# The first two query tiles of q and k by the hardware queues as token pairs, with a new load list and TensorE order

## The chip, the cores and the metric

The kernel runs on one core of one Trainium2 chip. The metric is the device time of one execution in microseconds, as the median of several runs. The profile shown is one execution on that core.

## The reference

Attention with a local window, a few global keys and a linear distance bias, for 4 batches, 8 heads, 768 tokens and a head size of 64, then a feed-forward layer with squared ReLU over 3072 tokens (512 to 2048 to 512). n_global is 8, n_local is 96.

```python
scores = scale * np.matmul(q, k.transpose(0, 1, 3, 2))
is_global = pos[None, :] < int(n_global)
is_local = (rel >= 0) & (rel < int(n_local))
keep = is_global | is_local
dist = np.where(is_global & ~is_local, float(n_local), np.abs(rel).astype(np.float32))
scores = scores - slopes[:, None, None] * dist[None, :, :]
scores = np.where(keep, scores, -1000000000.0)
a = np.exp(scores - np.max(scores, axis=-1, keepdims=True))
a = a / (np.sum(a, axis=-1, keepdims=True) + 1e-09)
attn_out = np.matmul(a, v).astype(np.float32)
x = attn_out.transpose(0, 2, 1, 3).reshape(B * S, H * D)
h = np.maximum(x @ w_in, 0.0)
out = h * h @ w_out
```

## The kernel before

A batch has six query tiles of 128 tokens. Because the window is 96 tokens long and the global keys are the first 8, a query tile needs only two key tiles: its own ("o") and the one before it ("b"), in which the first 32 rows are replaced by those of tile 0 (`kb` for keys, `vb` for values; tile 1 uses tile 0 itself). Three query tiles make a "half"; there are eight halves. The feed-forward layers of one half run on TensorE between the attention steps of the next. Only the first batch is done tile by tile, in an opening of about 25 us; it is what the change touches.

Everything is recorded as operations of a planner, `Plan`. TensorE's operations and the loads of GpSimd keep the order in which they are listed. For the first batch these orders are written by hand in two strings, OPENING and LOADING. The operations of the other engines are put into an order, and given to ScalarE (ACT) or VectorE (DVE), by the planner's costs and due times; on the chip every engine then works through its own fixed order. Where the planner expects TensorE to wait in the opening, `warm` fills the time with matmuls on a zero tile (L217 and L220).

The names in OPENING, for query tile r and half i of the four head pairs:

- `Tr`: `turn_tile`, transposes of a tile of q and k by TensorE into PSUM (L663), eight 128x128; two copies `qk<-trp` bring them to SBUF, and two more (`kb`) build the key tile with the global rows.
- `Sro`, `Srb`: `score_tile`, eight score matmuls of 64 rows (L696). For the tiles 0 to 2 eight more matmuls put the distance bias in (L689), and ACT's exp gives the weights at once; for tiles 3 to 5 VectorE multiplies by a mask after the exp (L717).
- `Ari`: `attend_tile` (L735), and on VectorE the reciprocal of the row sum and the scaling (L745 and L747, "norm" below).
- `Xri`: `tile_to_x`, two transposes (L762), copied into `xt`.
- `Vr`: `fix_v`, two VectorE copies for `vb` (L206). It is no TensorE operation; VectorE does it when its turn comes and waits there for the load.
- `Fc`, `Gci`, `Dc`, `Eci`: pieces of the first layer (L557) for the first tile, the second and third tiles, and the tiles of the second half; `c` is the chunk of w_in that they need.

PSUM is taken from two rings: six large buffers (`big`, for T, S, F, G) and two small ones (`att`, for A and X).

The names in LOADING are tiles of 128 tokens of q, k and v, and the chunks c0 to c3 of w_in. They are cast to float16 by the transfer (L316, L364), whose contiguous piece is one head of one token, 256 bytes. Tile 0 of q and k alone comes by the hardware queues of SP and ACT in float32, in one transfer each (L354), and is cast by VectorE (`sq<-rsq`, `sk<-rsk`). The loads of w_out follow (L371), then those of the next batch.

```python
OPENING = """T0 V2 S0o T1 A00 A01 S1b T2 S1o S2b S2o X00 A11 A10 X11 T3 X10 T4 V1 X01 A20 S3o S3b A21 F0
X20 S4o X21 S4b T5 A30 A31 V3 G01 S5b G00 F1 X30 G11 A41 A40 S5o V4 G10 G20 G21 X41 X31 F2
G31 X40 F3 A50 A51 E10 E01 G30 X50 X51 E11 E00 D0 D1"""
LOADING = """v1 k1 v0 q1 k2 q2 k3 v2 k4 q3 q4 c0 k5 q5 v3 c1 v4 c2 c3 v5"""
```

Of the kernel before, what the change touches and what calls it, by code (L numbers as in the profile page):

```python
# [8 lines left out]
FP32 = mybir.dt.float32  # L9
FP16 = mybir.dt.float16  # L10
# [3 lines left out]
P = 128  # L14
# [2 lines left out]

OPENING = """T0 V2 S0o T1 A00 A01 S1b T2 S1o S2b S2o X00 A11 A10 X11 T3 X10 T4 V1 X01 A20 S3o S3b A21 F0  # L20
X20 S4o X21 S4b T5 A30 A31 V3 G01 S5b G00 F1 X30 G11 A41 A40 S5o V4 G10 G20 G21 X41 X31 F2
G31 X40 F3 A50 A51 E10 E01 G30 X50 X51 E11 E00 D0 D1"""

LOADING = """v1 k1 v0 q1 k2 q2 k3 v2 k4 q3 q4 c0 k5 q5 v3 c1 v4 c2 c3 v5"""

# [29 lines left out]
class Plan:  # L59
# [10 lines left out]
    def __init__(self, warm_from, warm_until):  # L70
        self.warm_from, self.warm_until = warm_from, warm_until
        self.queues = {"PE": [], "LOAD": []}
        self.rest = []
        self.free = {e: 0.75 for e in ("ACT", "DVE", "POOL", "SP")}
        self.landed = 3.4
        self.rank = 0

    def pe(self, cost, emit, needs=(), takes=(), lag=0.24):
# [76 lines left out]
def kernel(  # L155
# [11 lines left out]
    nc = tc.nc  # L167

    B, H, S, D = q.shape
    NG, NL = int(n_global), int(n_local)  # L170
    d_model, d_ff = moe_w_in.shape
    NT = S // P
    NPAIR = H // 2
# [5 lines left out]
    GR = 32  # L179
# [7 lines left out]
    stage_p = ctx.enter_context(tc.tile_pool(name="stage", bufs=2))  # L187
# [4 lines left out]
    y_p = ctx.enter_context(tc.tile_pool(name="yp", bufs=6))  # L192
    ps_big = ctx.enter_context(tc.tile_pool(name="ps_big", bufs=6, space=bass.MemoryType.PSUM))
    ps_att = ctx.enter_context(tc.tile_pool(name="ps_att", bufs=2, space=bass.MemoryType.PSUM))

    plan = Plan(1.0, 24.0)
    big, att = Ring(6), Ring(2)

    def eng(e):
        return {"ACT": nc.scalar, "DVE": nc.vector, "POOL": nc.gpsimd}[e]  # L200

    def copy(e, out, in_):
        if e == "ACT":
            nc.scalar.copy(out=out, in_=in_)  # L204
        else:
            eng(e).tensor_copy(out=out, in_=in_)  # L206
# [5 lines left out]
    def warm(ps):  # L212
        fp32 = ps.dtype == FP32
        n = min(512, ps.shape[-1]) if fp32 else P
        for _ in range(int(plan.spare / (n / 2400 + 0.003))):
            if fp32:
                nc.tensor.matmul(ps[:, 0:n], lhsT=zero[:, 0:P], rhs=zero[:, 0:n], start=True,  # L217
                                 stop=True)
            else:
                nc.tensor.transpose(out=ps[:, 0:n], in_=zero[:, 0:P], identity=ident)  # L220
# [3 lines left out]
    ident = const.tile([P, P], FP16, name="ident")  # L224
# [72 lines left out]
    def behind(dma, first):  # L297
        tc.add_manual_dep(dma.ins, first.ins.name, mybir.DependencyInfo(
            mybir.DependencyClass.Sync, mybir.DependencyReason.DATA), reason="in turn")

    def staged(x, name):
        if getattr(x, name, None) is None:
            setattr(x, name, stage_p.tile([P, HT, H, D], FP16, name=name, tag=name))
        return getattr(x, name)

    def list_loads(x):
        r0 = x.half * HALF
        prev = halves[x.hb - 2] if x.hb >= 2 else None
        before = (prev.turned if prev else []) + ([*halves[x.hb - 1].turned, prev.x_ops[NPAIR - 1]] if x.hb > 3 else [])
        vbefore = [halves[x.hb - x.half - 3].attended[-1]] if x.hb >= 4 else []  # L310

        def rows(src, name, t, rank=None):
            def emit(e):
                dst = (x.bt.v[:, x.half * HT + t, :, 0:D] if name == "v"
                       else staged(x, name)[:, t, :, :])
                dma = nc.gpsimd.dma_start(out=dst, in_=src[x.b, :, r0 + t * P:r0 + (t + 1) * P, :]  # L316
                                          .rearrange("h p d -> p h d"))
                if x.hb > 3 and name == "sq" and t == 0:
                    for turn in halves[x.hb - 1].turns + halves[x.hb - 2].turns[-1:]:
                        behind(dma, turn)  # L320
                if name == "sk":
                    x.last_load = dma
            return plan.load(0.86, emit, vbefore if name == "v" else before, rank,
                             1.6 if x.hb == 0 else 2.6)

        if x.half == 0:
            def start(e):
                new_batch(x.bt)
                nc.vector.memset(x.bt.v[:, :, :, D:D + 1], 1.0)
            x.bt.op = plan.add({"DVE": 0.1}, start, vbefore, rank=0)  # L330
        if x.hb > 1:
            x.q_in = [rows(q, "sq", t) for t in range(HT)]
            x.k_in = [rows(k, "sk", t) for t in range(HT)]
            x.v_in = [rows(v, "v", t) for t in range(HT)]
        else:
            x.k_in, x.q_in, x.v_in = [None] * HT, [None] * HT, [None] * HT
            for t in range(HT):
                r = x.half * HT + t
                if r > 0:
                    for src, name, key, ops in ((k, "sk", "k", x.k_in), (q, "sq", "q", x.q_in)):  # L340
                        load_jobs[f"{key}{r}"] = lambda src=src, name=name, ops=ops, t=t: (
                            ops.__setitem__(t, rows(src, name, t, -3 if not plan.queues["LOAD"]
                                                    else None)))
                load_jobs[f"v{r}"] = lambda t=t: (
                    x.v_in.__setitem__(t, rows(v, "v", t)), x.v_in[t].needs.append(x.bt.op))
            return
        for l in x.v_in:
            l.needs.append(x.bt.op)
        x.bt.v_in = [*getattr(x.bt, "v_in", []), *x.v_in]


    def first_tile(x, dst, src, eng, e, lag):
        raw = stage_p.tile([P, H, D], FP32, name="r" + dst, tag="r" + dst, bufs=1)
        op = plan.add({e: 0.5}, lambda e: eng.dma_start(  # L354
            out=raw, in_=src[0, :, 0:P, :].rearrange("h p d -> p h d")), rank=-1)
        op.lag = lag

        def emit(e):
            copy(e, staged(x, dst)[:, 0], raw)
        return plan.add({"DVE": 0.42, "ACT": 0.54}, emit, [op], rank=0)  # L360

    def load_w_in(c):
        n = d_ff // 4
# [286 lines left out]

    def turn_tile(r):
        x, t = halves[r // HT], r % HT
        bt = x.bt
        st = {}

        def emit(e):
            st["ps"] = trp = ps_big.tile([P, 2, NPAIR, P], FP16, name="trp0", tag="big")
            warm(trp.rearrange("p i a c -> p (i a c)"))  # L660
            for i, src in enumerate((x.sq, x.sk)):
                for a in range(NPAIR):
                    nc.tensor.transpose(out=trp[:, i, a, :], in_=src[:, t, 2 * a:2 * a + 2, :],  # L663
                                        identity=ident)
        job = plan.pe(8 * 0.07, emit, [x.q_in[t], x.k_in[t], ident_op], [big])
        ops = [plan.after(job, {"ACT": 0.51, "DVE": 0.36}, lambda e, i=i: copy(
            e, bt.qk[:, i, r], st["ps"][:, i])) for i in range(2)]
        x.turned.append(job)
        tile_ops[r] = ops
        if 0 < r < NT - 1:  # L670
            def fix(e):
                copy(e, bt.kb[:, :, r - 1, GR:P], bt.qk[:, 1, r, :, GR:P])
                copy(e, bt.kb[:, :, r - 1, 0:GR], bt.qk[:, 1, 0, :, 0:GR])
            kb_ops[r] = plan.add({"DVE": 0.65, "POOL": 1.2}, fix, [ops[1], tile_ops[0][1]])

    def score_tile(r, before):
        bt = batches[0]
# [119 lines left out]
    x0, x1 = halves[0], halves[1]  # L797
    tile_ops, kb_ops, tiles = {}, {}, {}
# [6 lines left out]
    list_loads(x1)  # L805
    for c in range(4):
        load_jobs[f"c{c}"] = lambda c=c: load_w_in(c)
    x0.k_in[0] = first_tile(x0, "sk", k, nc.scalar, "ACT", 3.8)
    x0.q_in[0] = first_tile(x0, "sq", q, nc.sync, "SP", 3.4)
    for name in LOADING.split():  # L810
        load_jobs[name]()
    batches[0].v_in = x0.v_in + x1.v_in
    ident_op = plan.add({"DVE": 0.25}, fill_ident, [index], rank=0)
# [3 lines left out]
                           rank=0) for h in range(H)]  # L817
# [3 lines left out]

    jobs = {}
    for r in range(NT):
        jobs[f"T{r}"] = lambda r=r: turn_tile(r)
        jobs[f"V{r}"] = lambda r=r: fix_v(batches[0], r, r + 1)
        jobs[f"S{r}o"] = lambda r=r: score_tile(r, False)
        jobs[f"S{r}b"] = lambda r=r: score_tile(r, True)
        for i in range(2):
            jobs[f"A{r}{i}"] = lambda r=r, i=i: attend_tile(r, 2 * i)
            jobs[f"X{r}{i}"] = lambda r=r, i=i: tile_to_x(r, 2 * i)  # L830
    for c in range(4):
# [3 lines left out]
        for i in range(2):  # L835
            jobs[f"G{c}{i}"] = lambda ms=ms, i=i: layer1(x0, ms[2 * i:2 * i + 2], P, HALF)
            jobs[f"E{c}{i}"] = lambda ms=ms, i=i: layer1(x1, ms[2 * i:2 * i + 2], 0, 2 * P)
    for name in OPENING.split():
        jobs[name]()
    for job in l1(x1, 8) + l2(x0)[:6]:  # L840
        job()
    for hb in range(1, NHB):
        x = halves[hb]
# [51 lines left out]
```

## Time and profile before

| what | value |
|---|---|
| median of 5 runs | 217.09 us (216.98 to 217.22) |
| profiled execution | 217.22 us, of which the span from first to last instruction 215.4 us |
| granted TensorE clock | 0.997 of full speed |
| TensorE busy | 207.9 us, filler included |
| VectorE, ACT busy | 119.8 us, 119.6 us |
| GpSimd's queue | 77024 packets, 80.5% of the 16 engines' time over the span |
| SP's hardware queue | 30304 packets, 25.5% |
| ACT's hardware queue | 1040 packets, 0.6% |

PE is TensorE, PEld its weight loads, DVE VectorE, POOL GpSimd. Lines of the timeline give the start, the duration (of a group: from its first start to its last end), the engine, the line and the operation, and in brackets how long the engine was idle before and what ended that. Lines of the chain give a start, a duration and what the time was spent on. Of a DMA queue the profile gives packets, megabytes, and the time that its packets took as a share of 16 engines over the window asked for.

### The profile page before, as it was taken

How to read it: one execution, taken by the hardware profiler on the slowest of the kernel's cores; microseconds unless marked ns; L12 is line 12 of the kernel's file. 1: busy time of each engine (PE TensorE's matmuls, PEld its weight loads, DVE VectorE, ACT ScalarE, POOL GpSimd, SP SyncE). 2: the span in 40 equal slices, each digit the busy share in tenths (PEclk: the TensorE clock that was granted, in tenths of full speed). 3: DMA queues.
4: the chain of work that ended last, by engine and by line, in shares of the span. 5: the costliest groups of instructions: out<-in, count | busy, mean ns of one | idle time of the engine just before them, and what ended most of it. 6: DMA issues, size and time to landing. Idle time of an engine off the chain costs nothing.

```text
span 215.4 us, 4772 instructions
## 1 busy us (share of the span) xinstructions
PE 207.9 (97%) x1905; PEld 127.4 (59%) x1905; DVE 119.8 (56%) x340; ACT 119.6 (56%) x242; POOL 68.5 (32%) x84
## 2 busy tenths in 40 slices
PE   6979999999999999999999999999999999999994
PEld 7757899755455566446554565455654565456553
DVE  7458987433664489509880589319870697114300
ACT  7788986745661686138721785148721884137421
POOL 8997434486000760086006800086000000000000
PEclk9999999999999999999999999999999999999998
DMA  7999999999993799699936997199952101320012
GB/s 119 144 147 177 199 199 209 175 155 170 104 236 107 129 152 131 129 149 169 186 68 102 190 125 154 43 145 178 141 123 97 52 0 37 88 97 0 0 53 97
DMA packets 108391, 26.80 MB, mean 124 GB/s; under 512 B 101072, under 2 KB 105424, under 8 KB 108368
## 3 DMA queue, kind: packets, MB, share of 16 engines
q0 software_dynamic: 77024, 13.37, 80.5%
q1 hardware_dynamic: 30304, 12.85, 25.5%
q10 hardware_dynamic: 1040, 0.26, 0.6%
q8 instruction: 15, 0.25, 0.5%
q14 instruction: 8, 0.07, 0.1%
HBM read 27.26 MB, written 6.29 MB: 156 GB/s over the span
## 4 chain that ended last, share of the span: by engine, by line
PE 87%; ACT 3%; POOL 3%; DMA 3%; DVE 2%; issue 0%; POOLq 0%
PE hps L557 39%; PE yps L606 37%; PE sp L459 4%; PE av L516 4%; DMA v<-in_v_dram 3%; PE yps L634 2%; POOL sk L316 1%; ACT ex L709 1%; ACT qk L204 1%; POOL v L316 1%; POOL sq L316 1%; PE av L735 1%; DVE vb L206 1%; PE trx L762 0%; PE trp L406 0%; ACT xt L204 0%
## 5 line engine op out<-in xcount | busy, mean ns | idle before, releaser
L557 PE MATMUL hps<-xt,w_in_sb 128*128 128x384 f16 (+2 forms) x608 | 88.7, 301 | 0.0
L606 PE MATMUL yps<-w_out_sb,h 128*128 128x512 f16 x368 | 83.0, 379 | 0.0
L557 PEld LDWEIGHTS <-w_in_sb 128*128 128x128 f16 x608 | 53.5, 98 | 26.5
L581 ACT ACTIVATE hr<-hps 128x384 f16<-128x384 f32 (+1 forms) x97 | 49.7, 513 | 17.7 <-PE hps L557 15.0
L606 PEld LDWEIGHTS <-h 128*128 128x128 f16 x368 | 34.9, 98 | 39.0
L204 ACT COPY y<-yps 128x512 f32<-128x512 f32 (+1 forms) x25 | 14.2, 569 | 67.1 <-PE yps L606 64.6
L592 DVE TENSOR_TENSOR h<-hr 128x768 f16<-128x768 f16 (+1 forms) x70 | 35.5, 520 | 24.5 <-ACT hr L581 24.3
L316 POOL DMA_DIRECT2D sq<-in_q_dram x23 | 20.6, 905 | 69.1 <-DMA xt<-tm 65.5
L583 DVE TENSOR_SCALAR hr<-hps 128x384 f16<-128x384 f32 x25 | 13.9, 556 | 37.9 <-PE hps L557 37.0
L474 ACT ACTIVATE ex<-sp 128x512 f16<-128x512 f32 x66 | 34.1, 610 | 1.2 <-PE sp L459 1.2
L316 POOL DMA_DIRECT2D v<-in_v_dram x24 | 21.7, 927 | 4.8 <-DMA w_out_sb<-in_moe_w_out_dram 3.3
L316 POOL DMA_DIRECT2D sk<-in_k_dram x23 | 20.4, 903 | 3.8 <-DMA w_out_sb<-in_moe_w_out_dram 2.5
L494 DVE TENSOR_TENSOR phat<-ex,mask 128x1024 f16<-128x1024 f16 (+1 forms) x36 | 19.9, 595 | 1.9 <-ACT ex L474 1.9
L526 DVE TENSOR_TENSOR tm<-av,rec 128x384 f16<-128x384 f32 x24 | 13.4, 558 | 0.8
L206 DVE COPY vb<-v 128x520 f16<-128x520 f16 (+1 forms) x32 | 10.1, 318 | 3.0 <-DMA v<-in_v_dram 2.5
L516 PEld LDWEIGHTS <-phat 128*128 128x128 f16 x240 | 9.8, 98 | 3.1
L516 PE MATMUL av<-v,phat 128*128 128x65 f16 x144 | 10.9, 194 | 0.0
L459 PEld LDWEIGHTS <-qk 64*128 64x128 f16 x168 | 6.3, 94 | 6.7 <-issue 6.3
L516 PE MATMUL av<-vb,phat 128*128 128x65 f16 x96 | 10.2, 193 | 0.0
L459 PE MATMUL sp<-qk 64*128 64x128 f16 x168 | 9.8, 218 | 0.4 <-ACT ex L474 0.4
L206 DVE COPY kb<-qk 128x96 f16<-128x96 f16 (+4 forms) x56 | 8.4, 208 | 0.9 <-ACT qk L204 0.8
L206 DVE COPY qk<-trp 128x512 f16<-128x512 f16 (+1 forms) x10 | 3.9, 403 | 7.3 <-PE trp L406 4.4
(65 smaller groups left out, 136.4 us busy)
## 6 DMA issues: line engine op xcount, KB each, us to landing
out_dram<-y SPq DMA_DIRECT2D x23, 256.0 KB, 2.3
v<-in_v_dram POOLq DMA_DIRECT2D x24, 128.0 KB, 6.9
sk<-in_k_dram POOLq DMA_DIRECT2D x23, 128.0 KB, 6.3
sq<-in_q_dram POOLq DMA_DIRECT2D x23, 128.0 KB, 5.6
w_in_sb<-in_moe_w_in_dram POOLq DMA_DIRECT2D x4, 512.0 KB, 10.1
w_out_sb<-in_moe_w_out_dram POOLq DMA_DIRECT2D x4, 512.0 KB, 15.9
xt<-tm SPq DMA_TRANSPOSE x24, 2.4
rsk<-in_k_dram ACTq DMA_DIRECT2D x1, 256.0 KB, 4.4
```

The lines of the kernel that those rows point to most:

```text
L204: nc.scalar.copy(out=out, in_=in_)
L206: eng(e).tensor_copy(out=out, in_=in_)
L316: dma = nc.gpsimd.dma_start(out=dst, in_=src[x.b, :, r0 + t * P:r0 + (t + 1) * P, :] .rearrange("h p d -> p h d"))
L459: nc.tensor.matmul(sp[u][h][:, i, :], lhsT=lhsT, rhs=bt.qk[rows, 0, r, a, :], start=True, stop=True)
L474: nc.scalar.activation(out=st["ex"][:, h], in_=sp[u][h], func=AF.Exp, scale=scale)
L494: eng(e).tensor_tensor(out=x.phat[a][:, :, t0:t0 + n], op=ALU.mult, in0=st["ex"][:, :, i0:i0 + 2 * n].rearrange("p e (t b) c -> p e t (b c ...
L516: nc.tensor.matmul(av[:, h, j, :], lhsT=lhsT, rhs=rhs, start=not before, stop=before or r == 0)
L557: nc.tensor.matmul(st["ps"][:, i * n:(i + 1) * n], lhsT=w_in_sb[:, kk, m * P:(m + 1) * P], rhs=x.xt[:, kk, c0:c1], start=kk == 0, stop=kk ...
L581: nc.scalar.activation(out=o, in_=i, func=AF.Relu)
L583: eng(e).tensor_scalar(out=o, in0=i, scalar1=0.0, scalar2=None, op0=ALU.max)
L592: eng(e).tensor_tensor(out=x.h2[:, m0:m0 + width, c0:c1], in0=hr, in1=hr, op=ALU.mult)
L606: nc.tensor.matmul(st["ps"], lhsT=x.h2[:, m, j * P:(j + 1) * P], rhs=w_out_sb[:, m, :], start=m == 0, stop=m == NFT - 1)
```

## The change

Tiles 0 and 1 of q and k now both come by the hardware queues. Partition p receives the tokens 2p and 2p+1, which lie side by side in DRAM, so that a contiguous piece is 512 bytes. Each of q and k comes in two transfers of four heads (`first_tiles`), into buffers of the output pool `y_p`. The cast, one for each transfer, puts even and odd tokens apart, and the copies after the transposes put them together again, with a stride in PSUM. `turn_tile(0, 2)` does both tiles in two groups of eight transposes, the first for the head pairs 0 and 1, the second for 2 and 3, into two PSUM buffers.

GpSimd no longer loads k1 and q1. It loads v0 first, and c1 before c0. OPENING has a new order: T1 is gone, T2 follows T0, and F1 comes ahead of F0. The planner's time of the first landing on GpSimd's queue goes from 3.4 to 4.2, and with it the order on the other engines.

```diff
-OPENING = """T0 V2 S0o T1 A00 A01 S1b T2 S1o S2b S2o X00 A11 A10 X11 T3 X10 T4 V1 X01 A20 S3o S3b A21 F0
-X20 S4o X21 S4b T5 A30 A31 V3 G01 S5b G00 F1 X30 G11 A41 A40 S5o V4 G10 G20 G21 X41 X31 F2
-G31 X40 F3 A50 A51 E10 E01 G30 X50 X51 E11 E00 D0 D1"""
+OPENING = """T0 T2 S0o S1b A01 S1o A00 T3 S2b X01 S2o A10 A11 T4 S3b V1 X00 X11 A21 S4o A20 F1 X21 S3o
+X10 S4b X20 F0 G00 V2 T5 V3 V4 G11 A30 G10 A31 S5o G30 G31 S5b A41 G01 F3 X30 G21 A40 X31 F2
+X40 X41 G20 A50 E00 A51 E01 E11 X50 X51 E10 D0 D1"""
-LOADING = """v1 k1 v0 q1 k2 q2 k3 v2 k4 q3 q4 c0 k5 q5 v3 c1 v4 c2 c3 v5"""
+LOADING = """v0 k2 q2 k3 v2 v1 q3 v4 k4 q4 c1 c0 q5 k5 v3 c3 v5 c2"""
...
-        self.landed = 3.4
+        self.landed = 4.2
...
-                if r > 0:
+                if r > 1:
...
-    def first_tile(x, dst, src, eng, e, lag):
-        raw = stage_p.tile([P, H, D], FP32, name="r" + dst, tag="r" + dst, bufs=1)
-        op = plan.add({e: 0.5}, lambda e: eng.dma_start(
-            out=raw, in_=src[0, :, 0:P, :].rearrange("h p d -> p h d")), rank=-1)
-        op.lag = lag
-
-        def emit(e):
-            copy(e, staged(x, dst)[:, 0], raw)
-        return plan.add({"DVE": 0.42, "ACT": 0.54}, emit, [op], rank=0)
+    def first_tiles(x, dst, src, eng, e, lags):
+        casts = []
+        for i, lag in enumerate(lags):
+            hs = slice(i * H // 2, (i + 1) * H // 2)
+            st = {}
+
+            def start(e, hs=hs, st=st):
+                st["raw"] = y_p.tile([P, H // 2, 2, D], FP32, name="y", tag="y")
+                eng.dma_start(out=st["raw"].rearrange("p h j d -> p h (j d)"),
+                              in_=src[0, hs, 0:2 * P, :].rearrange("h (p j) d -> p h (j d)", j=2))
+            op = plan.add({e: 0.5}, start, rank=-1)
+            op.lag = lag
+
+            def emit(e, hs=hs, st=st):
+                copy(e, staged(x, dst)[:, 0:2, hs], st["raw"].rearrange("p h j d -> p j h d"))
+            casts.append(plan.add({"DVE": 0.42, "ACT": 0.54}, emit, [op], rank=0))
+        return casts
...
-    def turn_tile(r):
+    def turn_tile(r, n=1):
...
+        else:
+            half = plan.pe(0.56, lambda e: emit(e, (0, 1), True), [*first[::2], ident_op],
+                           [big] * 2)
+            job = plan.pe(0.56, lambda e: emit(e, (2, 3), False), first[1::2])
...
+        def evac(i, u):
+            def emit(e):
+                if n == 1:
+                    return copy(e, bt.qk[:, i, r], st[0][:, i])
+                c = slice(u * P // 2, (u + 1) * P // 2)
+                copy(e, bt.qk[:, i, u].rearrange("p a (c j) -> p a c j", j=2),
+                     st[i][:, :, :, c].rearrange("p j a c -> p a c j"))
+            op = plan.add({"ACT": 0.51, "DVE": 0.36 if n == 1 else 0.6}, emit, [job])
...
-    x0.k_in[0] = first_tile(x0, "sk", k, nc.scalar, "ACT", 3.8)
-    x0.q_in[0] = first_tile(x0, "sq", q, nc.sync, "SP", 3.4)
+    first = (first_tiles(x0, "sk", k, nc.scalar, "ACT", (3.8, 4.4))
+             + first_tiles(x0, "sq", q, nc.sync, "SP", (3.4, 4.3)))
...
-        jobs[f"T{r}"] = lambda r=r: turn_tile(r)
+        jobs[f"T{r}"] = lambda r=r: turn_tile(r, 2 if r == 0 else 1)
```

## The prediction

> **What bounds the kernel now.** I read the page's top first, then the chain of waits in order of time, the timeline of the first 34 us, and last the DMA view cut down to single issues.
>
> ```profile
> span 215.4 us, 4772 instructions
> PE 207.9 (97%) x1905; PEld 127.4 (59%) x1905; DVE 119.8 (56%) x340; ACT 119.6 (56%) x242; POOL 68.5 (32%) x84
> PE   6979999999999999999999999999999999999994
> ```
>
> TensorE is the bound, but its 97% counts filler: the first slices hold 57 matmuls on the zero tile. All its useful work is fixed by the change (same transposes, scores, attends, layers), so the end moves only with the time in which TensorE does nothing useful. The chain shows where that time is:
>
> ```profile
> 8.15 5.87 DMA v<-in_v_dram
> 14.05 0.31 DVE vb L206
> 14.38 0.80 DVE vb L206
> 15.19 0.65 DVE kb L206 x2
> 17.63 1.07 ACT qk L204 x2
> 18.98 1.97 ACT ex L709 x4
> 24.13 1.87 PE hps L557 x24
> ```
>
> From 24.1 us on the chain is TensorE nearly throughout. Before, it runs through a load (v2, issued 8.15, landed 14.03), the VectorE copies queued behind that load, and ScalarE. So this change is decided in the first 25 us. The timeline there:
>
> ```profile
> 5.89 0.47 PE L663 MATMUL trp<-ident,sq 128*128 128x128 f16 x4
> 8.15 0.84 PE L220 MATMUL trp<-ident,zero 128*128 128x128 f16 x12
> 8.83 0.40 PE L663 MATMUL trp<-ident,sq 128*128 128x128 f16 x4
> 11.18 0.40 PE L663 MATMUL trp<-ident,sq 128*128 128x128 f16 x4 [0.27 <-DMA sq<-in_q_dram]
> 15.92 0.25 PE L735 MATMUL av<-v,ph 128*128 128x65 f16 x3 [1.11 <-DVE rec L745]
> 19.27 1.06 PE L557 MATMUL hps<-xt,w_in_sb 128*128 128x128 f16 x16
> ```
>
> T0 starts at 5.89, T1 at 8.83 (q1 landed 4.51+4.3=8.81), T2 at 11.18 (q2 at 6.42+4.7), and one long hole ends at 15.92. Of the 24.06 us up to the end of S5b about 12.9 are useful work: T 0.46 a tile (six, 2.76), biased S 0.87 (five, 4.35), plain S 0.33 (five, 1.65), four attend matmuls 0.12 or 0.24 with a tile before (1.7), X 0.11 (six, 0.66), F0 0.90, G01 0.87. Some 11.2 us are not: 5.8 ahead of the first data, 5.4 in later holes. Those 5.4 are all that a better order could win.
>
> GpSimd's loads, by position in its list and landing time (issue plus landing): v1 6.4, k1 7.1, v0 8.1, q1 8.8, k2 10.2, q2 11.1, k3 12.1, v2 14.05, k4 14.7, q3 15.1, q4 16.4, c0 19.0, k5 20.0, q5 20.7, v3 21.8, c1 24.2, v4 25.1, c2 27.5, c3 30.2, v5 31.7: about 0.95 us a tile, 2.6 a weight chunk.
>
> **Part by part: loads.** Removed from GpSimd: k1 and q1, two issues of 0.90, so what follows stands two positions earlier. Added on SP and ACT: four issues in place of two (0.46 and 0.49 more), and 512 KB. SP's next work is at 49.7: free. ACT's table load and masks go back 0.49, less one slope (0.22) that passes to VectorE: hidden, because ACT then waits for the second half of k; 0.27 if that cover went.
>
> The same 2,080 packets now carry 512 B. The hardware queues' rows, first while they load q0 and k0, then for a 2 KB store near the end:
>
> ```profile
> q0 software_dynamic: 1038, 0.13, 37.4%
> q10 hardware_dynamic: 1040, 0.26, 21.6%
> q1 hardware_dynamic: 1040, 0.26, 20.9%
> ```
>
> ```profile
> q1 hardware_dynamic: 144, 0.26, 14.0%
> ```
>
> At its peak the first moved 289 GB/s, 14.2 ns for 256 B on each of 16 engines; the store took 14.0% of 5 us of 16 engines, 78 ns for 2 KB. On the line between, 512 B take 23.3 ns: estimated 130 x 23.3 = 3.0 us in place of 1.85. Counting from 2.25, the first halves are read by 3.8 and the second by 5.3 to 5.6 (GpSimd's packets come between). With the 0.5 and 1.0 us that q0 and k0 took from there to landing: halves of q at 4.3 and 6.1, of k at 4.8 and 6.6. Bounds for the second halves: 4.7 (packets cost no more for being larger) and 7.5.
>
> What does that do to GpSimd's queue? It starts about 4.1 us and moved 112 GB/s until 5.5, against 147 later: 0.35 us of slack in which hardware packets would cost nothing. The Trainium skill (DMA: Bandwidth & Descriptors, Issuing engines are not separate DMA queues) speaks against the change: DMAs from SP, ACT and GpSimd share the same 16 engines and interleave, so other queues save only issue time. By the rule, all 1.2 us of added transfer falls on GpSimd's loads; by the rows, about 0.85. I take 0.85 (ends 0.3 and 1.2). At 0.85, two removed tiles (1.9 us) bring in only 1.0. Expected: q2 9.0, k3 9.7, v2 11.05, v1 11.95, q3 12.95, v4 14.85, q4 15.95, c1 18.7, c0 21.2, k5 22.9, v3 23.9, c3 26.5, c2 30.1.
>
> **Casts and evacuations.** T0 now covers both tiles (16 transposes, 0.92), in two parts. k's second half is cast on ACT (about 0.59, the copy of 512 elements): 6.6 to 7.2; second part of T0 7.25 to 7.7. Behind it on ACT stand three masks (0.43 each) and then k's two evacuations (0.54): 9.05 and 9.6. On VectorE q's evacuations read PSUM with a stride. `qk<-trp` takes 422 ns for 512 elements, a plain float32 one (`hr`, 384) 556, so one element a cycle for 512 would be 0.69. The skill (VectorE: DVE Perf Modes, What auto-detection actually checks) grants two 16-bit elements a cycle only at step 1. The contiguous row would give 0.42, the rule 0.69; I take 0.69, 0.54 more for two. They end about 9.1, not after ACT: free here, up to 0.5 if ACT were earlier.
>
> **The path, step by step**, each engine in its new order. Spacings: ACT exp 0.50, qk 0.54, xt 0.28, hr 0.50; VectorE vb pair 0.85 (mean of 0.75, 1.14, 0.60, 0.61), kb pair 0.55, norm 0.62, qk 0.40, xt 0.33.
> - T2 at 9.0 (q2), S0o 9.46, S1b to 11.2. Before, S0o and T1 were done by 9.29; now T0 to T2, less work by 0.4 us (S0o's 0.87 missing, T2's 0.46 there).
> - A01 waits for S0o's second exp (11.55): 11.65. S1o to 12.64, A00, T3 at 13.0 (q3), S2b, X01, S2o to 15.3.
> - VectorE: vb for v2 and v1 until 13.3, norms until 14.55, T3's q until 14.95. ACT waits for that with nothing else in front: T3's k 15.54, S2b's exps and X01 until 16.82, S2o's until 17.8. So A11, which needs X01's buffer, runs at 16.4.
> - v4's vb, wanted only late, sits next on VectorE: it lands 14.85, copy to 15.8, kb 16.35, A1's norms 17.6, T4's q 18.0, ACT's k 18.6. S4o thus runs at 18.65 although T4 itself is done at 17.1. This is the old v2 block with another tile.
> - A20 19.45, F1 19.7 to 20.6, X21, S3o, X10 (A20's norm 21.27), S4b, X20 to 21.85; F0 to 22.75 (c0 at 21.2 is no wait), G00 23.67, T5 24.13, G11 25.0.
>
> The kernel before has the same useful work done at 24.06+0.96=25.02 (it is ahead by A30, A31, S5b and G01, 1.68, and lacks F1, G00 and G11, 2.64). So by 25 us the sum is 0. After it: A30, G10, A31, S5o to 26.9 (T5's evacuations on ACT end 26.5), G30 against c3 at 26.5, near 0.25 lost here. And a walk with mean steps is short: through the block from 14.05 to 15.92 the same method gives 15.3, 0.6 too early; I add 0.25 of that, as only one such block lies on the new path. Sum +0.5: 217.22 (the profiled execution, span 215.4 and 1.8 around it) to 217.7, and 217.6 against the median of 217.09, the profiled one standing 0.13 above it.
>
> Costed at nothing: w_out, landed by 41.2 and first read 45.6 (4 us of cover); the next batch's loads, landed by 49 and read from 50.6; the y buffers lent to the raw halves, wanted again at 49; the reordered kb, vb and qk copies near 51, whose loads are in by then. Each would cost its overrun.
>
> **The rivals.**
> - Faster: GpSimd's queue is delayed by 0.3 instead of 0.85, since the large packets run in its gaps. Then q2, q3, v4 and q4 come 0.55 sooner and so does the walk behind them, G30 finds c3 there (0.25), and v4's copy is done before A1's norms come, so the block's 0.25 leaves the path: 0.5-0.55-0.25-0.25=-0.55, 216.5. It decides from a delay under 0.4 (-0.45). For it: the slack at 4 to 5.5 us and two loads fewer. Against: latencies rise from 4.3 to 5.9 us by the eighth load, so the queue has no reserve later.
> - Nothing: holes only change place. v first buys nothing by itself: v0 lands near 7.2 and its first reader, A01, runs at 11.65. The walk's own result of about 0 stands: 217.1.
> - Slower by more: second halves at 7.5; T0's second part, k's evacuations, S0o and all exps behind slip 0.8: 218.3.
>
> **How the numbers follow.** The likeliest, slower near 217.6 (217.3 to 218.0): 0.40. Much slower: 0.08. Near nothing: 0.20. Faster: 0.32. A measurement here can tell about 0.2%, 0.43 us, from no change. So faster 0.32, same 0.20, slower 0.48. Range 216.2 (delay 0.3, second halves early, no friction) to 218.5.
>
> **What would show it.** Right: T0's second part after 7, T2 near 9, VectorE waiting for v4's vb near 14 to 15, S4o more than 1 us after T4, TensorE solid only after 22. Wrong: q2 landed by 8.4, no wait above 0.5 us between 13 and 20, or G11 ended before 24.5; then it is faster. A second part of T0 before 6.5 would refute the packet cost.

## The result, and the profile after

| what | before | after |
|---|---|---|
| median | 217.21 us (80 runs, 216.83 to 219.06) | 216.57 us (43 runs, 216.10 to 217.16) |
| ratio | | 0.9963 [0.9955, 0.9970] |
| profiled execution, span | 217.22 us, 215.4 us | 216.60 us, 214.8 us |

The changed kernel is faster by 0.64 us, 0.3%, by the medians. The ratio goes by all runs, and those of the kernel before reach up to 219 us, so by it the gain is 0.80 us (0.65 to 0.98). The forecast was half a microsecond up.

The page's top lines after the change:

```profile
span 214.8 us, 4782 instructions
PE 206.7 (96%) x1908; PEld 126.4 (59%) x1908; DVE 122.8 (57%) x343; ACT 119.6 (56%) x241; POOL 66.5 (31%) x82
PE   6698999999999999999999999999999999999994
```

TensorE still fills the span. The place where the time went is seen only in the chain of waits. First its opening, after the change (start, duration, what; lines of the same answer left out between them):

```profile
3.60 5.54 DMA sq<-in_q_dram
...
9.19 0.62 PE trp L675 x8
...
16.27 1.48 ACT ph L741 x3
...
21.86 1.77 PE hps L566 x24
```

The long load on the chain is no longer v2, issued at 8.15 and landed at 14.03, but q2, issued at 3.60 and landed at 9.14. (It is a close race: in other executions of this opening v2 stands there; see the opening's two forms below.) TensorE is solid from 21.9 us instead of 24.1. Yet all that this bought in this pair of executions is this: the first product of the second layer starts at 45.44, against 45.58 before. Now the chain behind that point, first of the kernel before, then of the changed one, with lines left out in between:

```profile
45.58 5.18 PE yps L606 x24
50.76 0.35 PE trp L406 x6
51.53 1.25 ACT qk L204 x3
52.82 0.49 PE trp L406 x6
55.60 3.56 PE yps L606 x16
```

```profile
45.44 5.18 PE yps L615 x24
50.62 0.67 PE trp L415 x12
52.16 0.67 PE trp L415 x12
55.11 3.56 PE yps L615 x16
58.67 0.34 PE sp L468 x7
59.03 0.61 ACT ex L483
```

From 45.58 to 55.60 are 10.02 us, from 45.44 to 55.11 are 9.67: 0.35 us go here, at the turns of the second batch's first half, where neither diff nor forecast had put anything. Before, the chain leaves TensorE for three copies of ScalarE (51.53), and the last turns wait for their end. From 55 us to the last copy both take the same (156.66 us; it starts at 212.26 and 211.77). So the profiled pair says: 0.14 us in the opening, 0.35 at 51 us.

Another 0.10 us lies behind the last copy, which is followed by 3.16 us in the kernel before and by 3.06 in the changed one. The last store lands at the same distance in both, 2.08 us. Then SyncE goes through a row of closing waits of about 0.06 us each, and three of these stand behind the wait for that store before, one after. So it is in every trace: 3.16 us in the four runs with the old opening and buffers, 3.03 to 3.06 in those built from the changed kernel. The three pieces make 0.59 of the 0.62 us between the two executions.

The timeline of the turns at 51 us, before and after (start, duration of the group, engine, operation, idle time and releaser):

```profile
51.13 0.36 DVE L206 COPY qk<-trp 128x384 f16<-128x384 f16 x1 [4.43 <-PE trp L406]
51.41 0.92 DVE L206 COPY vb<-v 128x520 f16<-128x520 f16 x2
51.53 1.63 ACT L204 COPY qk<-trp 128x384 f16<-128x384 f16 x4 [1.87 <-DVE qk L206]
52.82 0.33 PE L406 MATMUL trp<-ident,sq 128*128 128x128 f16 x3 [0.19 <-ACT qk L204]
```

```profile
47.21 0.70 DVE L206 COPY vb<-v 128x520 f16<-128x520 f16 x2 [0.65 <-DMA v<-in_v_dram]
48.23 0.83 DVE L206 COPY vb<-v 128x520 f16<-128x520 f16 x2 [0.31 <-DMA v<-in_v_dram]
51.00 1.24 ACT L204 COPY qk<-trp 128x384 f16<-128x384 f16 x3 [1.48 <-PE trp L415]
51.33 0.36 DVE L206 COPY qk<-trp 128x384 f16<-128x384 f16 x1 [2.27 <-PE trp L415]
```

Each turn fills one of the two small PSUM buffers and needs two copies, of q and of k, before the buffer is free. Before, VectorE took the first copy and then a vb copy of 0.92 us; so ScalarE got the next three copies, one behind the other, and could begin only at 51.53, behind VectorE's copy of the same turn. They ended at 52.78, and the fourth turn, which needs the buffer of the second, waited until 52.82. After the change, both vb copies have run by 49.1. ScalarE begins at 51.00 and is through with its three at 52.24; VectorE takes one beside it. No turn waits.

### The profile page after: what moved, and what is told of

The parts are those of the page before. It is cut to its first block, busy times and chain, and to the rows that moved or that the text cites. A ratio compares the mean times of both kernels' runs of the same rounds, so it can differ in the third digit from the quotient of the medians.

```text
span 214.8 us, 4782 instructions
## 1 busy us (share of the span) xinstructions
PE 206.7 (96%) x1908; PEld 126.4 (59%) x1908; DVE 122.8 (57%) x343; ACT 119.6 (56%) x241; POOL 66.5 (31%) x82
## 4 chain that ended last, share of the span: by engine, by line
PE 92%; DMA 3%; ACT 2%; POOL 1%; DVE 1%; issue 0%; POOLq 0%
PE hps L566 39%; PE yps L615 37%; PE sp L468 4%; PE av L525 4%; DMA sq<-in_q_dram 3%; PE yps L643 2%; PE sp L728 1%; PE sp L721 1%; PE av L767 1%; PE trp L675 1%; ACT ph L741 1%; PE trx L794 1%; PE trp L415 1%; POOL v L316 0%; ACT ex L741 0%; POOL sk L316 0%
## 5 line engine op out<-in xcount | busy, mean ns | idle before, releaser
L590 ACT ACTIVATE hr<-hps 128x384 f16<-128x384 f32 (+1 forms) x96 | 49.1, 512 | 18.4 <-PE hps L566 16.6
L316 POOL DMA_DIRECT2D sq<-in_q_dram x22 | 19.5, 897 | 68.1 <-DMA xt<-tm 66.2
L592 DVE TENSOR_SCALAR hr<-hps 128x384 f16<-128x384 f32 (+1 forms) x26 | 14.6, 561 | 37.4 <-PE hps L566 36.5
L316 POOL DMA_DIRECT2D sk<-in_k_dram x22 | 19.5, 904 | 4.8 <-DMA w_out_sb<-in_moe_w_out_dram 3.1
L206 DVE COPY vb<-v 128x520 f16<-128x520 f16 (+1 forms) x32 | 10.7, 336 | 2.5 <-DMA v<-in_v_dram 2.0
L204 ACT COPY qk<-trp 128x512 f16<-128x512 f16 (+1 forms) x12 | 6.2, 549 | 3.8 <-DVE qk L206 1.6
```

Of the source, the lines that this page charges most:

```text
L590: nc.scalar.activation(out=o, in_=i, func=AF.Relu)
L592: eng(e).tensor_scalar(out=o, in0=i, scalar1=0.0, scalar2=None, op0=ALU.max)
```

## Experiments: the turns at 51 us

To compare runs whose openings differ, I cut each profile's chain in stretches: the opening's end (start of the 24 second-layer products), the turns (to the next 16) and the scores (to the next 24). Behind the scores all took 146.07 us, within 0.01, to the last copy. The stretches are of one profiled execution each, which need not be the median one: that of c1 (216.77 us) was the slowest of six, those of l1 (217.72) and o2 (216.92) the fastest.

| run | median us | opening ends | turns | scores |
|---|---|---|---|---|
| before | 217.21 | 45.58 | 10.02 | 10.59 |
| after | 216.57 | 45.44 | 9.67 | 10.59 |
| m1 | 216.95 | 45.97 | 9.66 | 10.59 |
| m2 | 216.56 | 45.42 | 9.66 | 10.59 |
| m3 | 216.80 | 45.11 | 10.02 | 10.59 |
| o1 | 216.14 | 44.83 | 9.66 | 10.59 |
| o2 | 217.14 | 45.75 | 9.66 | 10.59 |
| l1 | 218.24 | 46.55 | 9.67 | 10.59 |
| b1 | 215.98 | 45.43 | 9.67 | 10.19 |
| m4 | 216.90 | 46.35 | 9.67 | 10.19 |
| c1 | 215.87 | 45.91 | 9.66 | 10.19 |
| c2 | 215.83 | 45.15 | 9.66 | 10.19 |

**m1: VectorE's vb copies ahead of the turns, in the old kernel.**

```diff
 # kernel before, fix_v
-                      wait=0.0 if bt is batches[0] else 4.0)
+                      wait=0.0 if bt in batches[:2] and t1 < HT + 1 else 4.0)
```

> The kernel before with one number changed: the conversions of v to fp16 of the second batch may stand as early as those of the first (their wait of 4.0 us behind the load in the planner's reckoning is 0), so that VectorE's two pairs of vb copies stand ahead of the first qk copy of the turns at 51 us, as they do in the changed kernel. Loads, TensorE's order and the opening are those of before. Theory A (most of the gain is made at the turns near 51 us, by VectorE's order and not by the loads): 0.35 us off, 216.7 to 216.9 beside 217.2; the chain shows the second group of turns without an idle gap near 52.8. Rival B (the gain is made by the opening: pairs of 512 bytes, two loads of GpSimd fewer, v first): no change, 217.1 to 217.3.

216.95 us beside 217.34 for the kernel before, ratio 0.9980 [0.9967, 0.9994]. The turns took 9.66 us, 0.36 less, and the stretches behind took what they took before. Theory A holds for the turns: the gain is to be had with no change to any load. The copies are shared out differently from the changed kernel, though: VectorE makes both q copies of the first two turns and ScalarE both k copies, where in the changed kernel VectorE makes one of the four and ScalarE three.

```profile
51.52 0.69 DVE L206 COPY qk<-trp 128x384 f16<-128x384 f16 x2 [0.35 <-PE trp L406]
51.91 0.86 ACT L204 COPY qk<-trp 128x384 f16<-128x384 f16 x2 [1.87 <-DVE qk L206]
```

What neither has is a row of three on ScalarE that begins late. The profiled opening of m1 ended at 45.97 with the very instructions of before, 0.39 later: this opening varies from execution to execution, which comes back below.

**m2: the old order of the turns in the changed kernel, a miss.** The second batch's vb copies wait 4.6 us in the planner, and the engines of the qk copies are fixed.

```diff
 # changed kernel
-                      wait=0.0 if bt is batches[0] else 4.0)
+                      wait=0.0 if bt is batches[0] else 4.6 if bt is batches[1] and t1 < HT + 1 else 4.0)
...
-            return plan.after(job, {"ACT": 0.39, "DVE": 0.31}, emit)
+            return plan.after(job, {"A": {"ACT": 0.39}, "D": {"DVE": 0.31}}[("DA", "AA", "DA", "DA")[a][i]], emit)
```

> The changed kernel with the order of before at the turns near 51 us: the second batch's vb copies wait 4.6 us in the planner's reckoning and the first qk copy of each pair of turns goes to the engine it had before, so that VectorE does the qk copy and then vb, and ScalarE begins behind it. Opening, loads and TensorE's order are those of the changed kernel. Theory A: 0.35 us back on, 216.85 to 217.0 beside 216.55 for the changed kernel and 217.2 for the kernel before. Rival B: stays at 216.5 to 216.65.

216.56 us, as the changed kernel: neither the expected rise nor evidence for the rival. The timeline shows what I had built:

```profile
50.97 1.24 ACT L204 COPY qk<-trp 128x384 f16<-128x384 f16 x3 [1.48 <-PE trp L415]
51.31 0.36 DVE L206 COPY qk<-trp 128x384 f16<-128x384 f16 x1 [3.44 <-PE trp L415]
51.58 0.60 DVE L206 COPY vb<-v 128x520 f16<-128x520 f16 x2
```

The turns run in the order of head pairs 1, 3, 0, 2, so that the pattern put both copies of the first turn on ScalarE, which began at 50.97. One vb copy does stand between VectorE's copies, as before, and costs nothing. So it is not a vb copy between VectorE's that counts, but the time at which ScalarE's row of three can begin.

**m3: the same with the engines in the right order.** The wait is 5.4 and the pattern `("AD", "DA", "AD", "AA")`; everything else is as in m2.

> The changed kernel with the order of before at the turns of the second batch near 51 us, which the run m2 did not bring back: there both copies of the first turn stood on ScalarE, from 50.97 us on. Here VectorE takes the q copy of the first turn and then vb, and ScalarE takes the k copy behind it and both copies of the second turn, as in the kernel before; TensorE, SyncE and GpSimd are as in the changed kernel. Theory A (what counts is when ScalarE's run of three qk copies begins: 51.53 us in the kernel before, 51.00 in the changed one, and the fourth turn waits for its end): the gap of 0.3 to 0.4 us before the second pair of turns comes back, 216.9 to 217.0 beside 216.57. Rival B (the whole gain is the opening's): 216.5 to 216.65.

216.80 us. The turns took 10.02 us again, and the timeline is that of before, 0.47 us earlier:

```profile
50.66 0.36 DVE L206 COPY qk<-trp 128x384 f16<-128x384 f16 x1 [4.43 <-PE trp L415]
51.05 1.63 ACT L204 COPY qk<-trp 128x384 f16<-128x384 f16 x4 [1.87 <-DVE qk L206]
52.35 0.33 PE L415 MATMUL trp<-ident,sq 128*128 128x128 f16 x3 [0.19 <-ACT qk L204]
```

The median rose by 0.23 us on the changed kernel's, a little less than the 0.35 of the stretch; the two were not measured side by side, which the next runs mend.

**q_m1, q_m3, q_after: both openings with both orders of the turns, on one chip.** They are the kernels of m1, m3 and the changed one, unedited.

> Old opening, new order of the turns at 51 us (the kernel of the run m1 once more, on one chip with q_m3 and q_after). The stretches give 0.36 us for the turns: 0.25 to 0.45 below the kernel before, and its scatter of over 1 us kept, if that comes from the opening.

> New opening, old order of the turns (the kernel of the run m3 once more). If the opening holds 0.14 us, as the profiled pair shows: 0.1 to 0.2 us below before. If it holds 0.3 to 0.5 us in the median because the old opening mostly runs worse than in the profiled execution: 0.3 to 0.5 us below before, with runs within 0.4 us of each other.

> The changed kernel itself: the sum of the two, 0.5 to 0.85 us below before; 0.25 to 0.4 us below q_m3 and 0.15 to 0.5 us below q_m1.

| median us (runs) | old turns | new turns |
|---|---|---|
| old opening | 217.40 (48) | 216.91 (22) |
| new opening | 216.84 (22) | 216.25 (11) |

Ratios to before: q_m1 0.9975 [0.9958, 0.9991], q_m3 0.9974 [0.9960, 0.9987], q_after 0.9948 [0.9932, 0.9964]. The new turns are those of m1 in the upper row and those of the changed kernel in the lower. By the medians the turns are worth 0.49 and 0.59 us here, the opening 0.56 and 0.66, each uncertain by 0.3 to 0.4 us as the intervals say. The sum of the two single steps, 1.05, is near the 1.15 of both. Every one of these steps is larger than I had expected. For the turns the profiles are the safer measure: q_m3 and q_after were profiled with the same opening (45.10 and 45.11 us), and there 216.60 us went to 216.25, the 0.35 of the stretch. What the medians show above that is the opening, which does not run the same each time.

**The opening's spread.** The old opening ended at 45.58, 45.97, 45.74 and 46.35 us in its four profiled executions (before, m1, q_m1, m4), and different loads of GpSimd stand on their chains. In q_m1 it is v3, for which TensorE waits at 22.3 us (lines left out in between):

```profile
14.10 8.20 DMA v<-in_v_dram
22.44 0.64 PE av L735 x16
45.74 5.18 PE yps L606 x24
```

The new opening, in the six executions of kernels that keep it whole, came in two forms: its end was 45.42 to 45.44 us in after, m2 and b1, and 45.10 to 45.11 in m3, q_m3 and q_after. They part at VectorE's copies of vb for v2, here in after and, from the chain, in q_after:

```profile
11.07 1.19 DVE L206 COPY vb<-v 128x520 f16<-128x520 f16 x2 [0.18 <-DMA v<-in_v_dram]
```

```profile
5.37 5.48 DMA v<-in_v_dram
10.87 0.65 DVE vb L206
11.54 0.29 DVE vb L206
45.11 5.18 PE yps L615 x24
```

The second of the two copies took 0.70 us in the later form and 0.28 to 0.29 in the earlier; the normalisations, T3's copies and ScalarE's work behind it moved by the 0.3 us between the forms. Why one and the same copy takes longer is not shown. So the profiled pair of the result compares the later form of the new opening with the earliest of the four old ones, and its 0.14 us is small for that reason. It was typical there: both executions stand at their medians (217.22 beside 217.21, 216.60 beside 216.57). In q_after the execution of the earlier form stands at the median (216.25). There, from q_m1 to q_after, the end of the opening moved by 0.63 us, and the 0.10 behind the last copy comes on top. With the medians beside it (0.56 and 0.66), the opening holds at least as much as the turns in those runs.

The runs of before spread over 216.77 to 219.35, those of q_m1, with the same opening, over 216.42 to 217.78, those of q_after over 216.04 to 216.56. I had expected q_m3's runs to lie within 0.4 us of each other; four of them stood at 217.45 to 217.48, 0.9 above the lowest.

## Experiments: the opening

**o2: without the pairs of tokens.** Each of the four hardware transfers brings one tile of 128 tokens in pieces of 256 bytes.

```diff
 # changed kernel, first_tiles
-                eng.dma_start(out=st["raw"].rearrange("p h j d -> p h (j d)"),
-                              in_=src[0, hs, 0:2 * P, :].rearrange("h (p j) d -> p h (j d)", j=2))
+                eng.dma_start(out=st["raw"].rearrange("p h j d -> p (h j) d"),
+                              in_=src[0, :, i * P:(i + 1) * P, :].rearrange("h p d -> p h d"))
```

> The changed kernel without the pairs of tokens: each of the four transfers of the hardware queues brings one tile of 128 tokens of all eight heads in pieces of 256 bytes, the cast copies it straight, the copies from PSUM are contiguous. Queues, loads left to GpSimd and the orders of all engines stay. Theory A (opening worth 0.15 us, of which the pairs are a small part): the transfers take 0.4 to 0.8 us longer together and the two VectorE copies from PSUM about 0.25 us less each; the first tile's half can still start as early, so -0.1 to +0.2 us, 216.45 to 216.8. Rival B (512-byte pairs make the gain): +0.3 us or more, 216.9 upward.

217.14 us, 0.57 above the changed kernel, and level with the kernel before (ratio 0.9994 [0.9986, 1.0002]) although its turns took the good 9.66 us: rival B is right that the opening's gain needs the pairs. (The edit changes with them which part of the two tiles comes first.) The chain:

```profile
3.59 6.14 DMA sq<-in_q_dram
9.78 0.62 PE trp L675 x8
```

q2 was issued at the same time and landed 0.59 us later. By 5.5 us the two hardware queues had moved 0.86 MB, against 0.98 in the changed kernel, and no packet of GpSimd's queue had gone in either: its loads start behind them. VectorE's two copies, contiguous here, took 0.76 us together against 1.29: that is free, as forecast.

**o3 and o4: the two removed loads put back, as copies that nobody reads.**

```diff
 # changed kernel, behind the load of v0 (o4)
+                for i, n in enumerate((k, q) if x.hb == 0 and name == "v" and t == 0 else ()): nc.gpsimd.dma_start(out=spare[:, i], in_=n[0, :, P:2 * P, :].rearrange("h p d -> p h d"))
```

> The changed kernel with two loads more on GpSimd's queue, right behind the first v tile: k1 and q1 come once more, into a tile that nobody reads, so that this queue again carries as many tiles ahead of q2 as before. Everything else stays. Each later landing should move about 1.9 us (two tiles at 0.95 us): q2 from 9.1 to 11.0, v4 from 13.8 to 15.7. Theory A: TensorE has other work for little of that; the turn of tile 2 waits for q2 and the whole opening moves by 1 to 1.9 us, 217.6 to 218.4. Rival (the two loads fewer are hidden as in my forecast's working, since the turns of tile 2 could wait): under +0.3 us, 216.5 to 216.8.

> The run o3 with its fault mended: there both extra loads wrote the same tile, so the second waited for the first to land and GpSimd issued nothing from 2.70 to 7.97 us. Here k1 and q1 come once more into two halves of a tile that nobody reads, without a wait. Each later landing should move about 1.9 us (two tiles at 0.95 us): q2 to about 11.0. If the landing of q2 sets the opening: +1.5 to +2 us on the changed kernel, 218.1 to 218.6. If there is slack behind it, as my forecast's working had for the loads of two tiles: under +0.5, 216.6 to 217.1.

o3 gave 223.21 us and is no measure of two loads: both wrote one tile, and on the chain stands `2.70 5.27 DMA spare<-in_k_dram`, GpSimd waiting for the first to land. o4 gave 219.55 us, 2.98 above the changed kernel and above its own expectation. q2 landed at 11.02, the 1.9 us expected. The rest goes with TensorE's clock: from T2 through the first four groups of scores the chain took 3.72 us in place of 2.28, of which some was won back later. The rows of the stretches 0 to 11, 11 to 15 and 15 to 20 us (after the five engines' busy times: granted clock, DMA share, GB/s), then the scores' bias matmuls at 11 to 15 us in o4 and at 9 to 13 us in the changed kernel (busy, mean ns, idle):

```profile
0.00:11.00 11.00, 6.77 (x69) 6.69 (x69) 7.58 (x24) 7.08 (x16) 9.96 (x17) 1.00 1.50 170
11.00:15.00 4.00, 3.94 (x43) 3.23 (x44) 2.18 (x7) 1.86 (x4) 4.00 (x6) 0.59 2.45 156
15.00:20.00 5.00, 5.00 (x103) 4.25 (x102) 3.50 (x14) 4.41 (x10) 4.03 (x5) 1.00 1.51 195
```

```profile
L722 PE MATMUL sp<-dmask,slope_id 128*128 128x128 f16 x16 | 2.1, 312 | 0.0
```

```profile
L721 PE MATMUL sp<-dmask,slope_id 128*128 128x128 f16 x24 | 1.8, 219 | 0.0
```

TensorE stood idle for 2.62 us ahead of T2 and then had 0.59 of its clock in the mean. With T2 right behind T0, the new order has nothing to do in a wait for q2; it is good only as long as q2 is early. In the changed kernel the same wait was 1.11 us, and the clock stayed at 1.00.

**l1: the new transfers under the old orders of TensorE's opening and of the loads.** OPENING is that of before without T1, LOADING that of before without k1 and q1.

> The changed kernel's transfers of the first two tiles by the hardware queues as pairs of tokens, under the old order of TensorE's opening and the old order of GpSimd's loads (k1 and q1 left out of it, since they now come with the first tiles; the two turns of T0 stand together). It tells what the transfers do without the two new orders. GpSimd's later loads come two tiles earlier (v2 near 12.2 in place of 14.05 us). If the opening's gain comes from the two loads that went: 0.3 to 1.5 us below before with its stalls at 51 and 59 us kept, 215.7 to 216.9. If the new orders are what turns the earlier loads to account: 217.0 to 218.0, since A00 then waits longer for v1 and v0, which start only behind the hardware queues' 1 MB.

218.24 us, ratio to before 1.0048 [1.0036, 1.0061], although the turns at 51 us took the good order here too. v2 landed at 11.84 instead of 14.03, and the opening ended at 46.55 against 45.58. In the timeline tile 0's first plain scores:

```profile
9.64 0.40 PE L728 MATMUL sp<-qk 64*128 64x128 f16 x8 [0.66 <-DVE qk L206]
```

In the kernel before they run at 7.82 us. As pairs, tile 0 is ready no sooner than tile 1, and VectorE makes its q copies only from 8.92 to 10.2, behind a vb copy that had waited for v0 until 8.35; in the kernel before tile 0's q copy was done by then (6.62 to 7.04). Everything behind it in the old order moved. So the transfers alone cost time; with the new orders, which have T2 ahead of the first scores, they pay. What the new orders would do with the old transfers was not run.

**o1: v0 behind k2 and q2.**

```diff
-LOADING = """v0 k2 q2 k3 ...
+LOADING = """k2 q2 v0 k3 ...
...
-                            ops.__setitem__(t, rows(src, name, t, -3 if not plan.queues["LOAD"]
-                                                    else None)))
+                            ops.__setitem__(t, rows(src, name, t, None)))
```

> The changed kernel with k2 and q2 ahead of v0 on GpSimd's queue, nothing else of the loads changed; the planner then fills other gaps with warming matmuls and shifts some copies, so this is not one edit alone. q2 should land 0.95 us earlier, at 8.2 in place of 9.1, and v0 at 9.1, ahead of the first attention product at 11.9. If the time at which q2 lands sets the opening (as the run o2 says, where q2 landed 0.59 us later and the median rose by 0.57): 215.7 to 216.3. If later landings (v4, k4, q4, c0 unchanged) or the copies of VectorE and ScalarE between 16 and 20 us set it: 216.4 to 216.6.

216.14 us, 0.43 below the changed kernel's 216.57; T2 ran at 8.00 in place of 9.19 and the opening ended at 44.83, 0.28 before the earlier form of the changed kernel's and 0.61 before the later. v first is not free, it costs the place ahead of q2. The edit also let the planner shift filler and copies, so the gain is not of the load alone; and that T2 came 1.19 us earlier but the opening's end so little says that by then q2 no longer sets it (v2 stands on the chain of o1).

## Experiments: a better version

The changed kernel's chain has one more gap, at 59.03 (shown above): TensorE waits for ScalarE's exponentials, since the third group of scores stands right behind the second.

```diff
-PLACES = {2: (3, 7, 7, 7, 10, 11, 12, 1, 0, 1, 0),
+PLACES = {2: (3, 7, 8, 7, 10, 11, 12, 1, 0, 1, 0),
```

b1 is this edit in the changed kernel, m4 in m1's, c1 in o1's; c2 is c1 with v2 ahead of k3.

> The changed kernel with the third group of scores of the second batch's first half one place later (8 in place of 7), so that a second-layer product of TensorE lies between it and the scores whose exponential is waited for at 59 us; the planner moves the transposes by DMA on SyncE with it. If the wait of 0.65 us at 59.0 to 59.65 on the chain is real idle time of TensorE: 0.4 to 0.65 us off, 215.9 to 216.2. If the same wait turns up at a later group: 216.5 to 216.7.

> The kernel before with two constants of the plan changed and nothing of its loads or its opening: the run m1 (vb of the second batch may stand early) and the third group of scores one place later, as in the run b1. If the two stalls are independent of the opening: m1 took 0.26 to 0.39 us off and b1 0.59, so 216.2 to 216.4, which is below the changed kernel (216.57). If the score group's place works only behind the new opening: 216.8 to 217.0.

> The run o1 (k2 and q2 ahead of v0) with the score group's place of b1: TensorE's opening order is that of o1. If the two gains add (0.43 and 0.59 us beside the changed kernel's 216.57): 215.45 to 215.65. If the stall at 59 us had shrunk with the earlier opening: 215.7 to 216.1.

> c1 with v2 and k3 changed over on GpSimd's queue. In o1 the chain of waits runs through the landing of v2 at 11.91 us and VectorE's vb copies, the normalisations and the qk copy behind it; with v2 one place earlier that landing should be near 11.0. If that chain sets the opening by itself: 0.3 to 0.6 us below c1. If the next turn (T3, which needs k3 and q3; q3 stays where it is) or VectorE's queue sets it: within 0.15 us of c1.

b1: 215.98 us, 0.59 below the changed kernel, with the attends straight behind the scores:

```profile
58.66 0.55 PE sp L468 x16
59.21 0.41 PE av L525 x10
```

The stretch of the scores fell from 10.59 to 10.19 us, 0.40, and so did the profiled execution, from 216.60 to 216.20 with the same form of the opening. The rest of the 0.59 fits the forms: three of b1's six runs stand at 215.87 to 215.89, some 0.3 below that execution. m4: 216.90 beside 217.34, ratio 0.9987 [0.9971, 1.0003]. Both stretches were as short as in b1, but its runs spread from 216.41 to 218.19, and its profiled opening ended at 46.35. Whether the two constants alone beat the change is thus not settled. What its chain begins with tells where the old opening's spread can come from:

```profile
14.97 10.69 DMA w_in_sb<-in_moe_w_in_dram
```

A chunk of w_in landed at 25.66 us there, and TensorE waited for it. In the new list, two tiles shorter, the second of the first two chunks lands at 21.1 and nothing waits for it. This is one execution, an example and no proof. c1 gave 215.87 and c2 215.83 (ratio to before 0.9933 [0.9920, 0.9946]): o1's gain and b1's do not add up (215.55 would be the sum), and v2's place makes no difference. By their medians b1, c1 and c2 beat both kernels (217.34 to 217.50 for before beside them, 216.57 or, in q_after, 216.25 for the changed one). The intervals of their ratios (b1: 0.9932 [0.9908, 0.9956]) overlap with that of q_after, so that the 0.40 us of the stretch is the safer figure for what is won over the change. Among the three these runs do not choose.

## Why the prediction was wrong

- **"Costed at nothing: ... the reordered kb, vb and qk copies near 51, whose loads are in by then."** This step failed, and it is more than half of the profiled pair's gain: 0.35 of 0.62 us (m1, m3). I had asked whether the copies' inputs were late. They were not. What changed was who makes which copy, and when ScalarE can begin with its three. I had the kernel before's chain with `ACT qk` and the wait at 52.82 in hand, and could have priced its going at 0.3 to 0.4 us; it would have turned +0.5 into about +0.1, still not a gain; the steps below hold the rest.
- **"near 0.25 lost here" (G30 against c3).** c3 landed at 26.1, not 26.5, and G30 ran at 26.56 without a wait: 0.
- **"I add 0.25" for the block at v4.** There was no block: v4 landed at 13.8, not 14.85, and VectorE's copy ran at 14.80 behind the normalisations and T3's copy, without waiting for a load. S4o came at 18.43 instead of 18.65, A20 at 19.17 instead of 19.45. The term was a margin in one direction only, and wrong: 0.
- **The sum of 0 by 25 us** was 0.14 too high for the profiled pair. The steps were close: T2 9.19 (9.0), S0o 9.65 (9.46), A01 11.86 (11.65), T3 13.16 (13.0), F1 19.40 (19.7), F0 21.69 (21.85), G11's end 24.9 (25.0). But I walked one opening of each kind, as if an opening ran the same each time. In the profiled executions the old one's end ranges over 0.77 us and the new one's over 0.34, and from q_m1 to q_after it moved by 0.63.
- **GpSimd's delay of 0.85 us** was right for the first loads (v0 at 7.27, q2 at 9.1 against 9.0) and for the later ones (q4 16.0 against 15.95, c1 18.5 against 18.7, c0 21.1 against 21.2). v4, the eighth, alone came 1.05 us earlier than forecast. The forecast had carried over, by position in the list, a pause of the old trace: there the seventh load landed at 12.1 and the eighth at 14.05. In the new trace the pause stands one load later, v4 at 13.8 and k4 at 15.65. The block at v4 hung on this.
- **The rival "faster"** had the right size (216.5), in part by luck: its two dropped margins of 0.25 did drop out, but the 0.55 that it took from a shorter delay did not happen. In its place stand the 0.35 at 51 us, the 0.14 of the opening and the 0.10 behind the last copy, which neither it nor the main forecast had. Taken from +0.5, the two margins and these three give -0.59.
- **"v first buys nothing by itself"** held only half: o1 puts what it costs at up to 0.43 us, its other shifts included.
- **Right:** the second halves of q and k, put at 6.1 and 6.6, landed at 5.65 and 6.25; the strided copy, put at 0.69, took 0.64 us and was hidden; S4o ran some 1.25 us after T4. The 1.2 us of delay that the forecast worked out from the rule of interleaving was the upper end: position by position the first seven loads landed 0.7 to 1.2 us later, the first (7.27 in place of 6.4) 0.87.
- **Its signs** were mixed. T2 and S4o came as they should if it was right. The second part of T0 began at 6.58, before the 7 forecast, though not before the 6.5 that would refute the packet cost. VectorE did not wait for v4, and TensorE was solid just before 22. Of the three signs of being wrong one came: TensorE's longest wait between 13 and 20 us was 0.43.

## What to carry to other kernels

When a change feeds a planner other times, compare the order and the engine of every copy that frees a TensorE buffer, over the whole kernel and not only where the change was made, and price each wait of the old chain that could go: here that was about half of the result. When a kernel's runs spread over more than the effect, profile several executions of it and compare like with like: here the old opening ended anywhere from 45.58 to 46.35 us. An order that puts a load's first reader right behind the filler stands or falls with that landing: late data costs the wait and, here after 2.6 us of idling, the clock as well.

## What the runs showed of the hardware

- The hardware queues took all of the transfer rate while they ran. Up to 5.5 us of the changed kernel:

```profile
q1 hardware_dynamic: 1056, 0.52, 32.6%
q10 hardware_dynamic: 918, 0.46, 27.8%
```

  No packet of GpSimd's queue stands there, though its first load was issued at 1.67 us; before, with half as much on the hardware queues, that queue had moved 1038 packets by then. It is not the size of the packets: in o2, with the same 1 MB in pieces of 256 bytes, none had gone either. In 512-byte pieces the two queues ran at 317 to 354 GB/s, against 289 at their peak with 256 before and up to 293 in o2. The Trainium skill (DMA: Bandwidth & Descriptors, Issuing engines are not separate DMA queues) has the queues interleave; in this window they did not.
- An idle time of 2.62 us was enough to bring TensorE's clock down (0.59 over the next 4 us in o4), 1.11 us was not (1.00). The Trainium skill (TensorE: Matmul & The Clock Gate, Part 1) puts the loss at an idle window of about 3.4 us; this idle time was shorter. In the trace of o4 the granted clock fell at 10.90 us and rose again at 14.31, 3.41 apart, and the same length before the fall, from 7.49, still held 0.95 us of filler. So here a stretch of that length was not wholly idle.
- Two copies of one turn, from different parts of one PSUM tile, did not overlap when VectorE and ScalarE shared them: in the kernel before ScalarE's began at 51.53, 0.40 us behind VectorE's (51.13, 0.36 long), and the trace names VectorE's as what released it; in m3 0.39 behind. Whether the chip or only this program's waits ask for that is not shown. With both copies of a turn on one engine, as at 51.00 in the changed kernel, the other is free for the next turn.
